# A selective-state mixer and two MLPs: another bank, another order and one work list in the second MLP

## Chip, cores and metric

The kernel runs on one core of one Trainium2 chip, in one launch. The metric is the device time in microseconds, from the first to the last work of an execution. Lower is better.

## What is computed

A chunked state-space mixer (4 batches, 8 heads, 768 steps) gives 3072 tokens of width 256. Two MLPs follow, each from 256 to 2048 and back to 256:

```
h = x @ w_in
g = np.maximum(h, 0.0) + np.log1p(np.exp(-np.abs(h)))      # first MLP: softplus
x = g @ w_out
...
h = x @ w_in
g = h * (1.0 / (1.0 + np.exp(-1.702 * h)))                 # second MLP
return (g @ w_out).astype(np.float32)
```

Inputs and outputs are fp32 in the reference; the weights reach the kernel as 64-bit words.

## The kernel before

**Operands in two parts.** The matrix products run in the type fp32r. A value is kept as a high part (a copy into fp32r) and a low part (the value minus the high part), and a product is three matmuls of 128x128 by 128x512: high by high, and the two mixed ones. Three such matmuls on one output are called a *triple* here. `rnd` makes the high part of an activation on ScalarE (gh), `low` its low part on VectorE (gl).

**First MLP.** The tokens are cut into 6 chunks `c` of 512, the 2048 hidden units into 16 blocks `m`; the loop runs over `t = 16 c + m`, from 0 to 95. A step has `g1` (6 matmuls), a softplus on ScalarE, `rnd`, `low` and, two steps later, `g2` twice (6 matmuls): four triples in all. While chunk c is multiplied, the mixer makes chunk c+1 between these (scans on VectorE, products on TensorE, `at_m` on VectorE after each `at_cb`), up to t = 79; from t = 80 on there is none left.

**Second MLP.** It takes the chunks in pairs `p` (3) and the weights in 8 parts `q`; a *group* `G = 8 p + q` (24 of them) makes the hidden units of one part for two chunks with seven products instead of eight (Strassen's scheme in Winograd's form, with sums of blocks of the weights and of x made beforehand). Each product is a triple. Products 1 and 2 share a PSUM bank: product 1 is copied to `u_p` by ScalarE, then product 2 is added on top of it in the same bank. So product 2 cannot start before the copy has read the bank. VectorE adds: `u_1` = product 6 + `u_p`, `u_2` = product 7 + `u_1`, and in `make` product 5 + `u_2` (called add11 here), product 4 + `u_2` (add10), product 3 on top of 5 + `u_1` (add01). Product 3 goes onto product 5's bank and so waits for add11. `make` then has ScalarE do the activation and `rnd`. `l2()` takes the next entry of a queue: one triple of the second matrix (output sums `o`). Between the products stand `l2` calls: a group has 7 products and 8 `l2`, 15 triples, save the first, which has 13.

**Weight work.** A weight part of the second MLP is a *unit* (16; even ones are w_in parts, "2i", odd ones w_out parts, "2o"). `unit_steps` gives its steps, each for VectorE ("D") or ScalarE ("A"): scale A, three A, join D, sign D, and for 2i block sums and a split in two pieces (4 D and 2 A more), for 2o one split (A, D). `sign` also issues the load of the unit three further on, on SP. The inputs of a pair of chunks have a list of their own (`pair`: differences and splits). `run(jobs, which)` goes through the letters of `which` and, for each, does the next step of the first job whose head is of that engine; before, it looks at the first two unfinished jobs only. Before the change the units 0 and 1 and the first sums of pair 0 start at t = 69 and are brought to their end at t = 80; units 2 to 8 and the rest of pair 0 are run in t = 80 to 95, and what is left is done behind the loop; units 9 to 15 and pair 1 stand in groups 0 to 7, pair 2 in groups 8 on.

Each engine takes its instructions strictly in the order written. `finish` copies an ended output sum, for the second MLP into a buffer `ot`, and SP stores it: a buffer is free again when its store has landed. All `ot` come from one tag with two buffers, which the third difference of a pair uses too.

Of the kernel before, what the change touches and what calls it, by code (L numbers as in the profile page):

```python
# [9 lines left out]
F32 = mybir.dt.float32  # L10
# [11 lines left out]
P = 128  # L22
# [19 lines left out]
def mixer_two_mlps(ctx: ExitStack, tc: tile.TileContext, pack_p, pack_q, pack_s, pack_x, a_rows, consts, w1i, w1o, w2i, w2o, out):  # L42
# [383 lines left out]
    def finish(c, j):  # L426
        if c < NC:
            o = x2[:, c, j, :]
        else:
            o = hid.tile([P, TB], F32, tag="e", name=f"ot{c}_{j}", bufs=2)  # L430
        if j == 0 or c == 2 * NC - 1:
            nc.scalar.activation(o, acc[c][j], AF.Copy)
        else:
            nc.vector.tensor_copy(o, acc[c][j])  # L434
        if c >= NC:
            nc.sync.dma_start(out=out[j, :, (c - NC) * TB : (c - NC + 1) * TB], in_=o)

    W1 = (w1ih, w1il)
    with tc.manual_schedule():
# [228 lines left out]

        def run(jobs, which):
            for eng in which:  # L670
                for job in [j for j in jobs if j][0:2]:
                    if job[0][0] == eng:
                        job.pop(0)[1]()
                        break

        def second():
            second_home()
            low(NT - 1)
            units = [unit_steps(u) for u in range(9, 16)]
            first, then, srcs = pair_sums(1)  # L680
            pair = [first + pair_split(1, then, srcs)]
            queue = [(NT - 2, 0), (NT - 2, 1), (NT - 1, 0), (NT - 1, 1)]
            lo12 = None

            def l2():
                if not queue:
                    return
                t, j = queue.pop(0)
                if t < NT:
                    g2(t, j)  # L690
                    c, last = NC - 1, t % NF == NF - 1
                else:
                    g, f, ct = (t - NT) // 4, (t - NT) // 2 % 2, t % 2
                    d = tt[t]
# [5 lines left out]
                    assert not 4 <= g < 8 or not units[2 * g - 8]  # L700
                    wh, wl = (w2o[n][g % 8][:, f, o] for n in "hl")
                    nc.tensor.matmul(a, wl, d["gh"], start=first, stop=False)  # L702
                    nc.tensor.matmul(a, wh, d["gh"], start=False, stop=False)  # L703
                    nc.tensor.matmul(a, wh, d["gl"], start=False, stop=last)  # L704
                if last:
                    finish(c, j)

            u_p, u_1, u_2 = x2[:, 0, 0], x2[:, 0, 1], x2[:, 1, 0]
            for G in range(24):
# [8 lines left out]
                def bank(n):  # L718
                    return ps_h.tile([P, TB], F32, tag="h", name=f"p{n}_{G}")

                def product(n, dst, start=True):
                    assert not 5 <= G < 8 or not units[2 * q - 9]
# [12 lines left out]
                    rnd(key(f, ct))  # L735
                    queue.extend([(key(f, ct), 0), (key(f, ct), 1)])

                b1 = bank(1)
                product(1, b1)
                nc.scalar.activation(u_p, b1, AF.Copy)  # L740
                if lo12 is not None:
                    low(lo12)
                run(units, "DA")
                l2()
                b6 = bank(6)
                product(6, b6)
                nc.vector.tensor_add(u_1, b6, u_p)
                run(units, "DA")
                run(pair, "DA")
                l2()  # L750
                product(2, b1, start=False)
                make(0, 0, b1)
                if G:
                    l2()
                b7 = bank(7)
                product(7, b7)
                nc.vector.tensor_add(u_2, b7, u_1)  # L757
                low(key(0, 0))
# [16 lines left out]
                run(units, "DA")  # L775
                lo12 = key(0, 1)
                l2()
                l2()
# [4 lines left out]
        for t in range(NT):  # L783
# [79 lines left out]
                first, then, srcs = pair_sums(0)  # L863
                pair = [first + then]
            if t == (NC - 1) * NF:
                for job in (*pair, *units):
                    for _, f in job:
                        f()
                second_open()
                units = [unit_steps(u, nc.vector if u % 2 else nc.scalar) for u in range(2, 9)]  # L870
                pair = [pair_split(0, [], srcs)]
            if c == NC - 2 and m >= 5:
                run(units, "DA" if m % 2 else "DDA")
                run(pair, "D")
# [65 lines left out]
```

## Time and profile before

| | us |
|---|---|
| median of 3 runs | 597.04 (594.16 to 597.46) |
| the profiled execution's own time | 593.67 |
| its span, first to last instruction | 591.9 |
| TensorE busy | 568.9 |
| VectorE busy | 453.5 |
| ScalarE busy | 327.6 |

Rows give times from the start of the span. PE is TensorE, PEld its weight loads, DVE VectorE, ACT ScalarE, SPq the queue of SyncE. A row of the timeline has the start, the duration, the engine, the line, the operation, output and inputs, and in brackets the idle time before it and what ended it. Line L740 is the copy to `u_p`, L726 a product, L702 to L704 an `l2` of the second MLP, L732 the adds of `make`, L734 its activation, L419 `rnd`, L747 and L757 the adds to `u_1` and `u_2`, L811 the softplus, L655 the high part of a weight (`hi`), L122 `scale`, L131 `three`, L136 `join`, L141 `sign`, L432 and L434 `finish`, L83 every subtraction on VectorE.

### The profile page before, as it was taken

Reading aid. Unit: us, or ns where it says so; the run is one execution under the profiler, and the core shown is the slowest. Engines: PE = TensorE matmul, PEld = TensorE weight load, DVE = VectorE, ACT = ScalarE, POOL = GpSimd, SP = SyncE. Lnnn points to the kernel's source line nnn. Section 1 sums busy time; section 2 is a strip of 40 time slices with the busy share of each in tenths; the row PEclk is TensorE's granted clock in tenths of the full one; section 3 lists DMA queues with packets and bytes.
Section 4 is the critical chain, followed back from the end, with each engine's and each line's share of the span. In section 5 each row is a group of like instructions: output and inputs, shape, how many; then the busy total and the mean of one; then the engine's idle time right before and its main releaser. Section 6 shows DMA issues by size and latency. Waiting matters only on the chain.

```text
span 591.9 us, 8940 instructions
## 1 busy us (share of the span) xinstructions
PE 568.9 (96%) x3380; PEld 447.1 (76%) x3380; DVE 453.5 (77%) x686; ACT 327.6 (55%) x560; POOL 104.4 (18%) x95
## 2 busy tenths in 40 slices
PE   7899999999999999999999989999989999999996
PEld 5455667888888888877878767777768888888885
DVE  5999959998787976998688688887566766665654
ACT  2756534544344344544786776675565656564553
POOL 1011336444464443531000000000000000000000
PEclk9799999999999999999999999999999999999999
DMA  8867641433514336221123111000100000100001
GB/s 284 281 191 258 227 161 62 144 114 131 167 47 159 122 124 225 92 93 38 37 83 131 35 37 45 27 0 1 53 18 1 2 0 0 73 1 0 1 1 71
DMA packets 26570, 52.31 MB, mean 88 GB/s; under 512 B 3072, under 2 KB 8608, under 8 KB 26528
## 3 DMA queue, kind: packets, MB, share of 16 engines
q1 hardware_dynamic: 26528, 51.75, 25.6%
q8 instruction: 26, 0.43, 0.3%
q14 instruction: 16, 0.13, 0.1%
HBM read 48.40 MB, written 3.34 MB: 87 GB/s over the span
## 4 chain that ended last, share of the span: by engine, by line
PE 67%; DVE 18%; ACT 7%; DMA 4%; issue 3%; SPq 0%; POOL 0%; DVEq 0%; ACTq 0%; POOLq 0%
PE h L393 15%; PE p L726 15%; PE o L704 5%; PE o L702 5%; PE o L703 5%; PE o L412 4%; PE o L414 4%; PE o L413 4%; PE o L410 3%; DVE gl L83 3%; DVE L L246 2%; ACT gh L419 2%; ACT g L734 2%; DVE g L732 2%; PE y L332 2%
## 5 line engine op out<-in xcount | busy, mean ns | idle before, releaser
L83 DVE TENSOR_TENSOR gl<-g,gh 128x512 fp32r<-128x512 f32 x176 | 139.5, 794 | 32.8 <-ACT gh L419 32.3
L811 ACT ACTIVATE g<-h 128x512 f32<-128x512 f32 x96 | 57.0, 594 | 105.6 <-PE h L393 95.3
L419 ACT ACTIVATE gh<-g 128x512 fp32r<-128x512 f32 x176 | 111.3, 632 | 5.6
L734 ACT ACTIVATE g<-g 128x512 f32<-128x512 f32 x72 | 45.5, 631 | 69.1 <-DVE g L732 67.6
L393 PE MATMUL h<-xh,w1ih 128*128 128x512 f32 x192 | 80.8, 421 | 0.5 <-ACT xh L359 0.5
L393 PE MATMUL h<-xl,w1ih 128*128 128x512 f32 x192 | 76.0, 396 | 0.0
L246 DVE TENSOR_TENSOR_SCAN L<-abz,eye 128x1024 f32<-128x1024 f32 (+1 forms) x25 | 61.8, 2471 | 4.1 <-PE abz L236 4.1
L414 PE MATMUL o<-gl,w1oh 128*128 128x512 f32 x160 | 62.5, 391 | 0.8 <-DVE gl L83 0.8
L412 PE MATMUL o<-gh,w1ol 128*128 128x512 f32 x160 | 63.2, 395 | 0.0
L413 PE MATMUL o<-gh,w1oh 128*128 128x512 f32 x160 | 62.4, 390 | 0.0
L393 PE MATMUL h<-xh,w1il 128*128 128x512 f32 x192 | 60.1, 394 | 0.4 <-DVE w1il L83 0.2
L732 DVE TENSOR_TENSOR g<-p,x 128x512 f32<-128x512 f32 x72 | 48.8, 687 | 11.3 <-PE p L726 10.2
L86 POOL TENSOR_TENSOR rhs_bd<-tc,pk 64x512 fp32r<-64x512 f32 x32 | 53.0, 1657 | 1.2
L702 PE MATMUL o<-gh,w2ol 128*128 128x512 f32 x120 | 46.8, 390 | 0.6 <-DVE ot L434 0.6
L704 PE MATMUL o<-gl,w2oh 128*128 128x512 f32 x120 | 46.7, 389 | 0.0
L703 PE MATMUL o<-gh,w2oh 128*128 128x512 f32 x120 | 46.7, 389 | 0.0
L757 DVE TENSOR_TENSOR x<-p,x 128x512 f32<-128x512 f32 x24 | 16.6, 691 | 35.6 <-PE p L726 35.6
L393 PEld LDWEIGHTS h<-xh,w1ih 128*128 128x128 f32 x192 | 36.3, 189 | 9.8 <-issue 1.9
L393 PEld LDWEIGHTS h<-xl,w1ih 128*128 128x128 f32 x192 | 36.3, 189 | 9.5 <-issue 2.9
L393 PEld LDWEIGHTS h<-xh,w1il 128*128 128x128 f32 x192 | 36.2, 189 | 9.1 <-DVE w1il L83 1.2
L311 DVE TENSOR_TENSOR L<-cb,L 128x512 f32<-128x512 f32 x40 | 26.8, 680 | 12.6 <-PE cb L301 12.6
L414 PEld LDWEIGHTS o<-gl,w1oh 128*128 128x128 f32 x160 | 30.0, 188 | 8.0 <-DVE gl L83 1.7
(164 smaller groups left out, 1043.0 us busy)
## 6 DMA issues: line engine op xcount, KB each, us to landing
abz<-scr_z SPq DMA_DIRECT2D x22, 512.0 KB, 4.0
pk<-pack_s SPq DMA_DIRECT2D x16, 512.0 KB, 4.6
px<-pack_x SPq DMA_DIRECT2D x20, 320.0 KB, 2.9
wraw_1i<-w1i SPq DMA_DIRECT2D x8, 512.0 KB, 4.4
wraw_1o<-w1o SPq DMA_DIRECT2D x8, 512.0 KB, 4.2
wraw_2i<-w2i SPq DMA_DIRECT2D x8, 512.0 KB, 3.5
wraw_2o<-w2o SPq DMA_DIRECT2D x8, 512.0 KB, 3.2
out<-ot SPq DMA_DIRECT2D x12, 256.0 KB, 2.0
```

Of the source, the lines that this page charges most:

```text
L83: nc.vector.tensor_sub(o, x, y)
L246: nc.vector.tensor_tensor_scan(out=d["L"][:, h].rearrange("p h t -> p (h t)"), data0=d["abz"][:, h].rearrange("p h t -> p (h t)"), data1=e ...
L393: nc.tensor.matmul(h, w[:, k, f], x[:, k, :], start=(n == 0), stop=(n == 5))
L412: nc.tensor.matmul(a, w1ol[:, m, o], d["gh"], start=first, stop=False)
L413: nc.tensor.matmul(a, w1oh[:, m, o], d["gh"], start=False, stop=False)
L414: nc.tensor.matmul(a, w1oh[:, m, o], d["gl"], start=False, stop=last)
L419: nc.scalar.activation(d["gh"], d["g"], AF.Copy)
L702: nc.tensor.matmul(a, wl, d["gh"], start=first, stop=False)
L703: nc.tensor.matmul(a, wh, d["gh"], start=False, stop=False)
L704: nc.tensor.matmul(a, wh, d["gl"], start=False, stop=last)
L726: nc.tensor.matmul(dst, w, x, start=start and i == 0, stop=i == 2, skip_group_check=not start)
L732: nc.vector.tensor_add(d["g"], src, add)
```

## The change

Four things, all in the order or the place of work; the matmuls are the same ones.

1. Product 1 of a group gets a bank of its own (pool `ps_c`, one bank, which the mixer used before), and product 7 comes ahead of product 2: the order of products goes from 1, 6, 2, 7, 5, 4, 3 to 1, 6, 7, 2, 5, 4, 3. `low` of the first activation comes behind add11.
2. Weight and pair work of the second MLP is taken from one list at set places of a group (`behind`), in the groups 0 and 1 from all units, from group 2 on from the first unit, the pair, the second unit. `run` looks at the whole list it is given.
3. In the first MLP the work starts at t = 77 instead of 69, with 3 VectorE and 2 ScalarE steps in each t up to 95; nothing is brought to its end at t = 80. All `scale` steps are on ScalarE. What is left of the units goes on in the second MLP. The table of the activation is loaded ahead of group 0.
4. `finish`: every j = 1 copy is VectorE's and goes to another tag (two buffers); the very last copy is cut in two halves of 256 columns, one on VectorE and one on ScalarE, each with its own store.

```diff
             o = x2[:, c, j, :]
         else:
-            o = hid.tile([P, TB], F32, tag="e", name=f"ot{c}_{j}", bufs=2)
-        if j == 0 or c == 2 * NC - 1:
-            nc.scalar.activation(o, acc[c][j], AF.Copy)
-        else:
-            nc.vector.tensor_copy(o, acc[c][j])
...
+            pool, tag = (hid, "e") if j == 0 else (stg, "wt")
+            o = pool.tile([P, TB], F32, tag=tag, name=f"ot{c}_{j}", bufs=2)
+        parts = [slice(0, TB)] if (c, j) != (2 * NC - 1, 1) else [slice(0, TB // 2), slice(TB // 2, TB)]
+        for i, f in enumerate(parts):
+            if j == i:
+                nc.scalar.activation(o[:, f], acc[c][j][:, f], AF.Copy)
+            else:
+                nc.vector.tensor_copy(o[:, f], acc[c][j][:, f])
...
         def run(jobs, which):
             for eng in which:
-                for job in [j for j in jobs if j][0:2]:
-                    if job[0][0] == eng:
+                for job in jobs:
+                    if job and job[0][0] == eng:
...
-        def second():
+        def second(units):
             second_home()
+            nc.scalar.preload_act_table(AF.Gelu_apprx_sigmoid)
             low(NT - 1)
-            units = [unit_steps(u) for u in range(9, 16)]
+            units = units + [unit_steps(u) for u in range(len(units) + 2, 16)]
...
+            def behind(which):
+                jobs = [j for j in units if j]
+                run([*jobs[0:1], *pair, *jobs[1:2]] if G >= 2 else jobs, which)
...
-                b1 = bank(1)
+                b1 = ps_c.tile([P, TB], F32, tag="cb", name=f"p1_{G}")
                 product(1, b1)
                 nc.scalar.activation(u_p, b1, AF.Copy)
+                behind("D")
                 if lo12 is not None:
                     low(lo12)
-                run(units, "DA")
+                behind("AA")
                 l2()
                 b6 = bank(6)
                 product(6, b6)
+                behind("D")
                 nc.vector.tensor_add(u_1, b6, u_p)
-                run(units, "DA")
-                run(pair, "DA")
+                behind("DA")
+                l2()
+                b7 = bank(7)
+                product(7, b7)
+                nc.vector.tensor_add(u_2, b7, u_1)
+                behind("DADAD")
                 l2()
                 product(2, b1, start=False)
                 make(0, 0, b1)
                 if G:
                     l2()
-                b7 = bank(7)
-                product(7, b7)
-                nc.vector.tensor_add(u_2, b7, u_1)
-                low(key(0, 0))
-                run(units, "DAD")
-                l2()
                 b5 = bank(5)
                 product(5, b5)
+                behind("A")
                 make(1, 1, b5, u_2)
+                low(key(0, 0))
...
             if t == (NC - 1) * NF:
-                for job in (*pair, *units):
-                    for _, f in job:
-                        f()
                 second_open()
-                units = [unit_steps(u, nc.vector if u % 2 else nc.scalar) for u in range(2, 9)]
-                pair = [pair_split(0, [], srcs)]
-            if c == NC - 2 and m >= 5:
-                run(units, "DA" if m % 2 else "DDA")
-                run(pair, "D")
-            if c == NC - 1:
-                run(units, "DADA" if m % 2 else "DADAD")
-                run(pair, "DA")
-        for job in (*units, *pair):
-            for _, f in job:
-                f()
-        second()
+                pair[0] += pair_split(0, [], srcs)
+                units += [unit_steps(u) for u in range(2, 9)]
+            if t >= (NC - 1) * NF - 3:
+                run([*[u for u in units if u][0:1], *pair, *[u for u in units if u][1:2]], "DADAD")
...
+        second(units[2:])
```

How the order moves, first on ScalarE between the roundings of group 2 and the first activation of group 3 (`x2_100<-p1_3` is the copy to `u_p`). Before:

```order
L734 ACTIVATE g2_01_3772<-g2_01_3772 128x512
L419 ACTIVATE gh105_3775<-g2_01_3772 128x512
L655 ACTIVATE w1oh_98<-wt_2o5_3617 128x512
L740 ACTIVATE x2_100<-p1_3_3786 128x512
L131 ACTIVATE wraw_2i6_3547<-wraw_2i6_3547 128x512
L122 ACTIVATE wt_2o6_3804<-wraw_2o6_3641 128x512
L583 ACTIVATE w1oh_98<-t3_1_3509 128x512
L734 ACTIVATE g3_00_3813<-p1_3_3786 128x512
```

With the change:

```order
L745 ACTIVATE g2_01_3773<-g2_01_3773 128x512
L419 ACTIVATE gh105_3776<-g2_01_3773 128x512
L751 ACTIVATE x2_100<-p1_3_3786 128x512
L131 ACTIVATE wraw_2o6_3628<-wraw_2o6_3628 128x512
L658 ACTIVATE w1ih_96<-x2_100 128x512
L658 ACTIVATE w1ih_96<-sums_367 128x384
L745 ACTIVATE g3_00_3828<-p1_3_3786 128x512
```

The weight split that stood between the rounding and the copy to `u_p` now stands behind the copy.

Second, VectorE from a step behind the last add of group 0 to add11 of group 1 (`g1_11<-p5_1`). With the change:

```order
L141 SCALAR_TENSOR_TENSOR x2_100<-wraw_2o4_3397,x2_100 128x512
L83 TENSOR_TENSOR gl97_3601<-g0_01_3578,gh97_3581 128x512
L83 TENSOR_TENSOR w2ol_3106<-x2_100,w2oh_3104 128x512
L760 TENSOR_TENSOR x2_100<-p6_1_3611,x2_100 128x512
L136 SCALAR_TENSOR_TENSOR wt_2i5_3534<-wt_2i5_3534,wraw_2i5_3448 128x512
L765 TENSOR_TENSOR x2_100<-p7_1_3622,x2_100 128x512
L141 SCALAR_TENSOR_TENSOR wt_2i5_3534<-wraw_2i5_3448,wt_2i5_3534 128x512
L641 TENSOR_TENSOR sums_367<-wt_2i5_3534 128x128
L83 TENSOR_TENSOR wt_2i5_3534<-wt_2i5_3534 128x128
L83 TENSOR_TENSOR sums_367<-sums_367,wt_2i5_3534 128x128
L83 TENSOR_TENSOR sums_367<-wt_2i5_3534,sums_367 128x128
L743 TENSOR_TENSOR g1_11_3654<-p5_1_3649,x2_100 128x512
```

All weight steps of a group now stand ahead of add11, where before some stood among the adds that follow it, as in the next group of the kernel before:

```order
L732 TENSOR_TENSOR g2_11_3746<-p5_2_3742,x2_100 128x512
L732 TENSOR_TENSOR g2_10_3758<-p4_2_3754,x2_100 128x512
L83 TENSOR_TENSOR gl107_3763<-g2_11_3746,gh107_3749 128x512
L83 TENSOR_TENSOR w1ol_99<-x2_100,w1oh_98 128x512
L732 TENSOR_TENSOR g2_01_3772<-p5_2_3742,x2_100 128x512
```

Third, the last copies on ScalarE, with the semaphores each waits for. Before:

```order
L734 ACTIVATE g23_01_5552<-g23_01_5552 128x512 [waits DVE_49]
L419 ACTIVATE gh189_5555<-g23_01_5552 128x512 [waits PE_49,Activation_49]
L432 ACTIVATE ot10_0_5576<-o10_0_4995 128x512 [waits DMAHW2_49,PE_49]
L432 ACTIVATE ot11_0_5588<-o11_0_5010 128x512 [waits DMAHW4_49,PE_49,Activation_49]
L432 ACTIVATE ot11_1_5594<-o11_1_5011 128x512 [waits DMAHW3_49,DMAHW1_49,DMAHW5_49,DVE_49,PE_49]
```

With the change:

```order
L745 ACTIVATE g23_01_5553<-g23_01_5553 128x512 [waits DVE_49]
L419 ACTIVATE gh189_5556<-g23_01_5553 128x512 [waits PE_49,Activation_49]
L435 ACTIVATE ot10_0_5577<-o10_0_4996 128x512 [waits DMAHW0_49,PE_49]
L435 ACTIVATE ot11_0_5589<-o11_0_5011 128x512 [waits DMAHW2_49,PE_49]
L435 ACTIVATE ot11_1_5595<-o11_1_5012 128x256 [waits DMAHW7_49,DMAHW3_49,DVE_49]
```

The buffers of the last copies are now those of stores two output chunks earlier, and ScalarE's half of the last copy waits for VectorE, whose half stands first.

## Rows read from the trace of the kernel before

**Rows 1.** The page's part 1: busy time, share of the span, instructions.

```profile
PE 568.9 (96%) x3380; PEld 447.1 (76%) x3380; DVE 453.5 (77%) x686; ACT 327.6 (55%) x560; POOL 104.4 (18%) x95
```

**Rows 2.** Windows of 20 us in the second MLP: busy us (instructions), granted clock, DMA.

```profile
340.00:360.00 20.00, 17.78 (x76) 14.05 (x77) 16.11 (x28) 13.77 (x25) 0.00 (x0) 1.00 0.13 46
440.00:460.00 20.00, 20.00 (x90) 16.55 (x89) 13.14 (x21) 12.07 (x20) 0.00 (x0) 1.00 0.00 1
```

**Rows 3.** Waits of TensorE: us in total, times, longest.

```profile
PE p L726 <- ACT x L740: 6.0, 8, 1.4
PE cb L301 <- DVE L L311: 1.6, 2, 0.9
PE p L726 <- DVE g L732: 1.4, 2, 0.9
...
PE o L414 <- DVE gl L83: 0.8, 1, 0.8
```

**Rows 4.** Timeline, group 1: a weight split, the copy to `u_p`, product 2.

```profile
339.94 0.61 ACT L655 ACTIVATE w2oh<-x 128x512 fp32r<-128x512 f32 x1
...
340.46 0.58 ACT L740 ACTIVATE x<-p 128x512 f32<-128x512 f32 x1
...
341.09 0.50 PE L726 MATMUL p<-x2h,w2ih 128*128 128x512 f32 x1 [1.13 <-ACT x L740]
```

**Rows 5.** Timeline: product 1 of group 0, product 2 of group 3, product 1 of group 10, `u_p` twice.

```profile
327.05 0.39 PE L726 MATMUL p<-x2h,w2ih 128*128 128x512 f32 x1
...
364.00 0.50 PE L726 MATMUL p<-x2h,w2ih 128*128 128x512 f32 x1 [0.46 <-ACT x L740]
...
439.84 0.39 PE L726 MATMUL p<-x2h,w2ih 128*128 128x512 f32 x1
...
471.74 0.58 ACT L740 ACTIVATE x<-p 128x512 f32<-128x512 f32 x1
481.94 0.58 ACT L740 ACTIVATE x<-p 128x512 f32<-128x512 f32 x1
```

**Rows 6.** Timeline, VectorE in group 9: the copy of an output sum.

```profile
429.07 0.69 DVE L434 COPY ot<-o 128x512 f32<-128x512 f32 x1 [1.66 <-DMA out<-ot]
```

**Rows 7.** Timeline, ScalarE: the softplus of t = 55, 63, 79 and 95.

```profile
204.59 0.60 ACT L811 ACTIVATE g<-h 128x512 f32<-128x512 f32 x1 [2.46 <-PE h L393]
...
229.55 0.60 ACT L811 ACTIVATE g<-h 128x512 f32<-128x512 f32 x1 [2.46 <-PE h L393]
...
281.23 0.60 ACT L811 ACTIVATE g<-h 128x512 f32<-128x512 f32 x1 [2.53 <-PE h L393]
...
325.88 0.60 ACT L811 ACTIVATE g<-h 128x512 f32<-128x512 f32 x1 [0.96 <-PE h L393]
```

**Rows 8.** Timeline, ScalarE in group 0: `three`, the table load, the first activation.

```profile
328.97 0.65 ACT L131 ACTIVATE wraw_2o<-wraw_2o 128x512 uint32<-128x512 uint8 x1
329.64 1.28 ACT L734 ACT_TABLE_LOAD   x1
330.93 0.60 ACT L734 ACTIVATE g<-p 128x512 f32<-128x512 f32 x1
```

**Rows 9.** Timeline, VectorE: a block sum at t = 82, and two operations in group 1.

```profile
289.35 0.29 DVE L638 TENSOR_TENSOR sums<-wt_2i 128x128 f32<-128x128 f32 x1
...
340.67 0.68 DVE L83 TENSOR_TENSOR w2ol<-x,w2oh 128x512 fp32r<-128x512 f32 x1
341.27 0.68 DVE L747 TENSOR_TENSOR x<-p,x 128x512 f32<-128x512 f32 x1
```

**Rows 10.** Timeline at the end: TensorE's last matmul and the last copy.

```profile
586.49 0.39 PE L704 MATMUL o<-gl,w1oh 128*128 128x512 f32 x1
...
588.40 0.60 ACT L432 ACTIVATE ot<-o 128x512 f32<-128x512 f32 x1 [0.17 <-DMA out<-ot]
```

**Rows 11.** Loads of weights: the page's part 6, and all loads of line L110.

```profile
wraw_2i<-w2i SPq DMA_DIRECT2D x8, 512.0 KB, 3.5
...
DMA to landing us min/median/max: 3.1/3.8/9.2
```

More of the change, by code (lines that the diff above doesn't have):

```diff
@@ L429, in finish @@
         else:
-            o = hid.tile([P, TB], F32, tag="e", name=f"ot{c}_{j}", bufs=2)
-        if j == 0 or c == 2 * NC - 1:
-            nc.scalar.activation(o, acc[c][j], AF.Copy)
-        else:
-            nc.vector.tensor_copy(o, acc[c][j])
-        if c >= NC:
-            nc.sync.dma_start(out=out[j, :, (c - NC) * TB : (c - NC + 1) * TB], in_=o)
+            pool, tag = (hid, "e") if j == 0 else (stg, "wt")
[6 more added lines that the diff above has]
+                nc.vector.tensor_copy(o[:, f], acc[c][j][:, f])
+            if c >= NC:
+                nc.sync.dma_start(out=out[j, :, (c - NC) * TB + f.start : (c - NC) * TB + f.stop], in_=o[:, f])
     W1 = (w1ih, w1il)
@@ L670, in run, with ready @@
             for eng in which:
-                for job in [j for j in jobs if j][0:2]:
-                    if job[0][0] == eng:
+                for job in jobs:
+                    if job and job[0][0] == eng:
                         job.pop(0)[1]()
                         break
-        def second():
+        def second(units):
             second_home()
+            nc.scalar.preload_act_table(AF.Gelu_apprx_sigmoid)
             low(NT - 1)
-            units = [unit_steps(u) for u in range(9, 16)]
+            units = units + [unit_steps(u) for u in range(len(units) + 2, 16)]
             first, then, srcs = pair_sums(1)
             pair = [first + pair_split(1, then, srcs)]
+            def ready(u):
+                return not units[u - 2]
+            def behind(which):
+                jobs = [j for j in units if j]
+                run([*jobs[0:1], *pair, *jobs[1:2]] if G >= 2 else jobs, which)
             queue = [(NT - 2, 0), (NT - 2, 1), (NT - 1, 0), (NT - 1, 1)]
@@ L699, in l2 @@
                     last = g % 8 == 7 and f != ct
-                    assert not 4 <= g < 8 or not units[2 * g - 8]
+                    assert not 1 <= g < 8 or ready(2 * g + 1)
                     wh, wl = (w2o[n][g % 8][:, f, o] for n in "hl")
@@ L721, in product @@
                 def product(n, dst, start=True):
-                    assert not 5 <= G < 8 or not units[2 * q - 9]
+                    assert not 1 <= G < 8 or ready(2 * q)
                     wh, wl = (w2i[x][q][:, BLOCK[n] * P : BLOCK[n] * P + P] for x in "hl")
@@ L774, in second @@
                 low(key(1, 0))
-                run(units, "DA")
                 lo12 = key(0, 1)
@@ L865, in mixer_two_mlps @@
             if t == (NC - 1) * NF:
-                for job in (*pair, *units):
-                    for _, f in job:
-                        f()
                 second_open()
-                units = [unit_steps(u, nc.vector if u % 2 else nc.scalar) for u in range(2, 9)]
-                pair = [pair_split(0, [], srcs)]
-            if c == NC - 2 and m >= 5:
-                run(units, "DA" if m % 2 else "DDA")
-                run(pair, "D")
-            if c == NC - 1:
-                run(units, "DADA" if m % 2 else "DADAD")
-                run(pair, "DA")
-        for job in (*units, *pair):
-            for _, f in job:
-                f()
-        second()
+                pair[0] += pair_split(0, [], srcs)
+                units += [unit_steps(u) for u in range(2, 9)]
+            if t >= (NC - 1) * NF - 3:
+                run([*[u for u in units if u][0:1], *pair, *[u for u in units if u][1:2]], "DADAD")
+        import sys; print("AT END", len(pair[0]), [len(u) for u in units], file=sys.stderr)
+        for _, f in pair[0]:
+            f()
+        assert not units[0] and not units[1]
+        second(units[2:])
     ps_ctx.close()
```

## The prediction

> **What bounds the kernel now.** The page's first part shows TensorE busy 568.9 of 591.9 us [rows 1], so the kernel is bound by TensorE, and a gain can only come from stretches in which it waits, and from the two ends. The windows say where: in the second MLP it is busy 17.78 of 20 us between 340 and 360 and all of 20 between 440 and 460, at the full granted clock (1.00, the 2.4 GHz level) in both [rows 2]. TensorE's own waits name the releaser: eight waits, 6.0 us, for the copy to `u_p`, two for add11 or add01, and three in the first MLP for VectorE [rows 3]. The timeline of one shows why: a weight split stands on ScalarE ahead of the copy, and product 2 starts as the copy ends [rows 4].
>
> **What the stretch loses.** Between two copies of the steady part lie 10.20 us [rows 5], for 15 triples: 0.68 each. From product 1 of group 0 to that of group 10 the matmuls alone need 13 x 0.68 + 9 x 10.20 = 100.64 us; the trace has 439.84 - 327.05 = 112.79 [rows 5]. The loss is 12.15 us, more than the idle time in the waits, since a wait also empties the matmul pipeline (the first matmul behind it takes 0.50 us instead of 0.39 [rows 4, 5]).
>
> In the first MLP eight steps take 24.96 us (t = 55 to 63), so t = 63 to 79 should take 49.92 and took 51.68; t = 79 to 95 should take 16 x 4 x 0.68 = 43.52 and took 44.65 [rows 7]. That is 1.76 + 1.13 = 2.89 us lost there.
>
> **The change: groups 3 to 23.** Product 2 now starts 6 triples (4.08 us) into a group instead of 4 (2.72), and the copy no longer has a split ahead of it. Where VectorE is not late, product 3 of the group before starts at 8.16 and its sum is ready 0.89 later (0.45 to the start of its third matmul, 0.39 for that, 0.04 to the next engine), at 9.05; add01, activation, rounding and the copy follow in 0.6 to 0.7 us each, and the copy ends about 1.5 us into the next group: 2.5 us to spare. The next deadline is product 3, which starts 12 triples (8.16 us) into a group and needs add11. In front of add11 VectorE has up to 10 operations of a start-to-start 0.60 us (340.67 to 341.27) and four small ones of 0.3 [rows 9]. I laid the order of the built program on these durations. In group 3 add11 starts at 6.5 and is ready at 7.2, in group 4 (pair 1's split of 1024 columns) at 7.5, in group 8 (pair 2 and a copy of an output sum) at 7.9: all before 8.16. So no loss from group 3 on. The waits for stores in groups 8 and 9 (VectorE stood 1.66 us [rows 6]) go with the second tag. The new bank for product 1 is read last by the first activation, about 5.6 us into a group, and wanted again at 10.2.
>
> **Groups 0 to 2** carry most weight work, and are late in the new order too.
> Group 0 (0 is its product 1): ScalarE ends `three` of unit 8 at 0.8, the table at 2.05, the copy at 2.7; two splits, a `scale` and a `three` follow at 0.45 to 0.55 start to start, until 4.7. VectorE does join, sign and gl of t = 95 from 0.8, four sums to 3.7, `u_1`, `u_2`, two low parts, a join, and starts add11 at 6.6, ready 7.3. Product 3 could start after 10 triples, 6.8: 0.5 late, with 0.1 for the pipeline 0.6.
> Group 1: add01 of group 0 starts at 0.6 (VectorE waits for roundings before it), gl 1.2, sign 1.8, gl 2.7, low 3.75 (it waits for ScalarE's split), `u_1`, join, `u_2`, sign each 0.6 on, four sums to 7.85, then add11, ready 8.6 against 8.16: 0.5 lost.
> Group 2: likewise ready 8.5: 0.4 lost.
> Left: 1.5 us, so the gain here is 12.15 - 1.5 = 10.6. Bounds: 12.15, and 7 if groups 0 to 2 stay as they are (a rival, below).
>
> **First MLP.** With nothing brought to its end at t = 80 and VectorE free for the mixer until t = 77, the two waits on `at_m` go. At t = 78 `at_m` is still behind three moved steps, one of which waits for ScalarE's `three`; I get it ready 5.4 us after t = 77 began and wanted at 6.1. From t = 80 on a step has 2.72 us. VectorE has one gl and three steps, about 2.4 (4 x 0.60), ScalarE softplus, rounding and two steps, about 2.5, now with the three scales that VectorE did. Each load of a unit is issued some six steps ahead of its use, against 3.5 us to land [rows 11]. Both fit, but barely, and each can hold the other up, so I leave 0.5 of the 2.89: gain 2.4. Bounds: 2.9 and 0.
>
> **The end.** TensorE ends at 586.88; the last copy starts only at 588.40, behind stores, and ends at 589.0 [rows 10]. With the new tags it waits for no store. The halves do not run side by side: ScalarE's waits for VectorE's in the built order. Between 0.29 us for 128 columns and 0.69 for 512 [rows 6, 9] I take 0.4 for each, so the last ends at 587.75: gain 1.25. Bounds: 1.5 and 0.5. The stores behind it I leave as they are.
>
> **The table load** costs 1.28 us wherever it stands; before, it stood between product 2 and the first activation, now ahead of the copy, and is in the times of group 0 above. In the row it starts 0.02 us after the `three` before it ended, and the activation follows 0.01 us after it [rows 8].
> The Trainium skill, "ScalarE: Activation LUTs", section "What ACT_TABLE_LOAD costs", adds a drain of about 1.38 us to each load, 2.66 in all. By that the whole of ScalarE's list in group 0 would come 1.38 later.
>
> **Sum.** 10.6 + 2.4 + 1.25 = 14.2 us. Against the profiled execution's 593.67 that gives 579.5; the median shown is 3.4 above that execution, so 597.04 - 14.2 = 582.8.
>
> **Rivals.**
> 1. *VectorE and ScalarE stay too full at the seam.* For it: in the first MLP's last chunk both have 2.4 to 2.5 of 2.72 us, and every wait between them stops all that is queued behind. Then t = 77 to 95 and groups 0 to 2 lose what they lose now. Product 2 of group 3 stands at 364.00 [rows 5] and without waits at 327.05 + 8.84 + 20.40 + 2.72 = 359.01, so 5.0 of the 12.15 stay; the gain is 7.15 + 1.25 = 8.4: 588.6.
> 2. *A load lands late.* In group 1 ScalarE is to scale unit 12, whose load is issued by the sign of unit 9 in the same group (ready 2.5), with the activations of the group queued behind. At 3.5 us to landing [rows 11] the first rounding is ready at 8.5, wanted at 8.84, so past about 3.9 each us costs one. At the 9.2 of the slowest load [rows 11], which came in the busy first part of the kernel, that is 5.3: 588.1.
> 3. *The load of the table empties ScalarE first*, ahead of the copy and of all that is queued behind it. If that took as long as the load itself, 1.28 us [rows 8], and all of it came through to groups 0 and 1: 584.1. Against it: there is no such time in [rows 8]. The Trainium skill's rule on the drain, named above, is this rival.
> 4. *Slower: one bank for all first products.* Product 1 of each of 23 groups waits for the activation of the group before, where three rotating banks served. It decides from 10.2 us on; I find that activation at 5.6, in the early groups up to 7.2. To end 3 us above the median it would have to cost (14.2 + 3) / 23 = 0.75 us a group, so to end 5 us later than I find.
> 5. *No better than now*: that the change would not do what it says is ruled out by the order, in which the split stands behind the copy.
>
> **How the numbers follow.** Forecast 0.68, rival 1 0.17, rival 2 0.06, rival 3 0.05, rival 4 0.04. About 0.5% (3 us) is what a measurement of this kernel can tell from no change. Of rivals 1 and 2, 0.07 end within it, where new waits add to them. Faster: 0.68 + 0.05 + 0.16 = 0.89; same 0.07; slower 0.04. The range: with nothing lost anywhere the gain is 12.15 + 2.89 + 1.5 = 16.5, so 580.5, and the runs shown lie more below their median than above it, so 579.0; on the other side it takes in rivals 1 to 3 with some more, 589.5.
>
> **What would show it.** Right: no wait of TensorE for the copy to `u_p` from group 3 on, 10.2 us from group to group from there, waits of some tenths for add11 in groups 0 to 2, none on `at_m` in t = 72 to 77, the last copy ending within 0.9 us of the last matmul. Wrong: waits for add11 or a rounding in groups 3 to 9, gaps for gl in t = 80 to 95, ScalarE idle before a `scale` in group 1.

## The result and the profile after

The changed kernel took 580.4 us (median of 4 runs, 578.62 to 581.24) beside 595.78 for the kernel before (median of 4, 594.16 to 597.46): a ratio of 0.9738, 95% interval 0.9695 to 0.9781. Measured again later, it took 582.79 beside 597.51, with a ratio of 0.9754 (0.9728 to 0.9781). The forecast was 582.8, faster. It was reckoned down from 597.04, the median of the three runs that were shown; a fourth run lowered it.

Executions of one kernel begin at different paces (last section), so stretches are compared inside a trace. From the softplus of t = 63 to the end of the span the kernel before took 591.9 - 229.55 = 362.35 us [rows 7] and the changed one 579.4 - 231.40 = 348.0: 14.35 us less. Spans are shown to a tenth of a us, so the last digit of what is reckoned from one is uncertain. The 15.4 us between the two medians hold the start of the executions too.

Here are the page's part 1, then windows of 20 us (span; busy us and instructions of PE, PEld, DVE, ACT, POOL; granted clock, DMA share, GB/s), answering to [rows 1] and [rows 2]:

```profile
PE 568.5 (98%) x3380; PEld 452.7 (78%) x3380; DVE 453.1 (78%) x684; ACT 331.6 (57%) x563; POOL 102.4 (18%) x95
```

```profile
320.00:340.00 20.00, 19.49 (x86) 15.82 (x85) 16.05 (x29) 17.02 (x30) 0.00 (x0) 1.00 0.20 68
340.00:360.00 20.00, 19.03 (x82) 14.74 (x81) 17.68 (x32) 14.57 (x26) 0.00 (x0) 1.00 0.20 65
360.00:380.00 20.00, 20.00 (x90) 16.57 (x89) 19.00 (x33) 16.32 (x29) 0.00 (x0) 1.00 0.09 27
```

TensorE does the same 568 us of work in a shorter span. In the last of these windows it is never idle, though VectorE is busier there (19.00 of 20) than where TensorE waits. Of TensorE's waits (us in total, times, longest) the groups of [rows 3] on the copy, on `at_m` and on gl are gone; one is left of the second MLP:

```profile
PE p L737 <- DVE g L743: 1.5, 3, 0.6
```

These are product 3 waiting for add11 in groups 0, 1 and 2. In the timeline stand product 1 of group 0, the three waits, then product 1, the copy and product 2 of group 3, and product 1 of group 10:

```profile
325.38 0.39 PE L737 MATMUL p<-x2h,w2ih 128*128 128x512 f32 x1
...
332.86 0.73 PE L737 MATMUL p<-xo,w2ih 128*128 128x512 f32 x2 [0.51 <-DVE g L743]
...
343.96 0.73 PE L737 MATMUL p<-xo,w2ih 128*128 128x512 f32 x2 [0.61 <-DVE g L743]
...
355.09 0.73 PE L737 MATMUL p<-xo,w2ih 128*128 128x512 f32 x2 [0.36 <-DVE g L743]
...
357.26 0.39 PE L737 MATMUL p<-x2h,w2ih 128*128 128x512 f32 x1
...
358.93 0.58 ACT L751 ACTIVATE x<-p 128x512 f32<-128x512 f32 x1
...
361.34 0.39 PE L737 MATMUL p<-x2h,w2ih 128*128 128x512 f32 x1
...
428.66 0.39 PE L737 MATMUL p<-x2h,w2ih 128*128 128x512 f32 x1
```

In group 3 the copy ends at 359.51 and product 2 starts at 361.34, 4.08 us after product 1: 1.8 us to spare where [rows 4] show none. Product 1 of group 0 to that of group 10 (called *the ten groups* below) takes 428.66 - 325.38 = 103.28 us, against 112.79 in [rows 5]: 9.51 less. The softplus of t = 63, 79 and 95, answering to [rows 7]:

```profile
231.40 0.60 ACT L822 ACTIVATE g<-h 128x512 f32<-128x512 f32 x1 [2.46 <-PE h L393]
...
280.70 0.60 ACT L822 ACTIVATE g<-h 128x512 f32<-128x512 f32 x1 [0.80 <-PE h L393]
...
324.22 0.60 ACT L822 ACTIVATE g<-h 128x512 f32<-128x512 f32 x1 [0.38 <-PE h L393]
```

49.30 and 43.52 us, before 51.68 and 44.65: 3.51 less. At the end the two halves of the last copy, answering to [rows 10]:

```profile
575.32 0.39 PE L715 MATMUL o<-gl,w1oh 128*128 128x512 f32 x1
575.74 0.43 DVE L437 COPY ot<-o 128x256 f32<-128x256 f32 x1 [0.67 <-PE o L715]
576.20 0.38 ACT L435 ACTIVATE ot<-o 128x256 f32<-128x256 f32 x1 [0.54 <-DVE ot L437]
```

From TensorE's end to the end of the span pass 579.4 - 575.71 = 3.69 us instead of 591.9 - 586.88 = 5.02: 1.33 less. 9.51 + 3.51 + 1.33 = 14.35, the whole difference.

### The profile page after: what moved, and what is told of

Read it like the earlier page. It is cut to its first block, busy times and chain, and to the rows that moved or that the text cites. A ratio compares the mean times of both kernels' runs of the same rounds, so it can differ in the third digit from the quotient of the medians.

```text
span 579.4 us, 8939 instructions
## 1 busy us (share of the span) xinstructions
PE 568.5 (98%) x3380; PEld 452.7 (78%) x3380; DVE 453.1 (78%) x684; ACT 331.6 (57%) x563; POOL 102.4 (18%) x95
## 4 chain that ended last, share of the span: by engine, by line
PE 87%; DVE 7%; ACT 3%; issue 2%; DMA 1%; POOL 0%; DVEq 0%; POOLq 0%; ACTq 0%; SPq 0%
PE h L393 20%; PE p L737 17%; PE o L713 7%; PE o L714 7%; PE o L715 7%; PE o L412 6%; PE o L413 6%; PE o L414 6%; PE o L410 3%; PE y L332 2%; PE cb L277 2%; DVE L L246 2%; PE cb L301 1%; PE y L323 1%; PE abz L236 1%
## 5 line engine op out<-in xcount | busy, mean ns | idle before, releaser
L246 DVE TENSOR_TENSOR_SCAN L<-abz,eye 128x1024 f32<-128x1024 f32 (+1 forms) x25 | 63.3, 2534 | 3.9 <-PE abz L236 3.9
L745 ACT ACTIVATE g<-p 128x512 f32<-128x512 f32 x24 | 14.3, 594 | 49.9 <-PE p L737 49.8
L412 PEld LDWEIGHTS o<-gh,w1ol 128*128 128x128 f32 x160 | 30.0, 188 | 6.8 <-ACT gh L419 0.4
```

The costliest lines, as they stand in the source:

```text
L246: nc.vector.tensor_tensor_scan(out=d["L"][:, h].rearrange("p h t -> p (h t)"), data0=d["abz"][:, h].rearrange("p h t -> p (h t)"), data1=e ...
L412: nc.tensor.matmul(a, w1ol[:, m, o], d["gh"], start=first, stop=False)
L745: nc.scalar.activation(d["g"], src, AF.Gelu_apprx_sigmoid)
```

## The experiments

Times of single runs differ by some us from start to start, so verdicts rest on the stretches.

**1. The old order of products back.**

```diff
+                product(2, b1, start=False)
+                make(0, 0, b1)
+                if G:
+                    l2()
                 b7 = bank(7)
...
-                product(2, b1, start=False)
-                make(0, 0, b1)
-                if G:
-                    l2()
```

> The change with the old order of products (1, 6, 2, 7, 5, 4, 3); bank and work list stay new. Measured on the stretch from product 1 of group 0 to product 1 of group 10 (103.3 us in the changed kernel, 112.8 before). Theory, that the early copy to u_p or the late product 2 is enough, each alone: from group 3 on the copy ends 1.5 us into a group against 2.72 for product 2, so no wait for the copy there; but product 7 and u_2 come 1.36 us later, and add11 with them by up to 0.7: 104 to 106 us, with waits for add11. Rival, that the order of products is what brought the gain: waits for the copy in most of groups 1 to 7, 109 us or more.

The ten groups took 105.58 us, 2.30 more, within what the theory gave. As it had it, TensorE's waits are for add11, and none for the copy is long enough to be listed:

```profile
PE p L737 <- DVE g L743: 2.8, 4, 1.0
```

Groups 0 to 3 together take 42.1 us, as in the changed kernel; of the 2.30 us, 0.63 lie in group 4 and 1.53 in groups 8 and 9, where the next pair's work stands.

**2. Two ScalarE steps ahead of the copy again, in the new order.**

```diff
                 product(1, b1)
+                behind("AA")
                 nc.scalar.activation(u_p, b1, AF.Copy)
...
-                behind("AA")
```

> The change with the two ScalarE steps of the work list ahead of the copy to u_p instead of behind it; order of products and bank stay new. Theory: the copy ends 0.5 to 1.2 us later, still before product 2 at 4.08 us into the group: within 0.8 us of the changed kernel's 103.3 us for groups 0 to 9, no waits for the copy from group 3 on. Rival, that the place of the steps is what brought the gain: waits for the copy of 0.4 to 1.1 us in groups 1 to 7, 107 us or more.

The ten groups took 104.12 us, 0.84 more, a little over what was allowed. There is one wait for the copy (0.54 us, group 1), the wait for add11 in group 0 has grown to 1.09, and there is nothing from group 3 on:

```profile
PE p L737 <- DVE g L743: 1.1, 1, 1.1
PE p L737 <- ACT x L752: 0.5, 1, 0.5
```

**3. Both undone.**

The two diffs together.

> The change with both undone: old order of products and two ScalarE steps ahead of the copy; the bank and the rest of the list stay new. Theory: the waits for the copy come back in groups 1 to 7, and the stretch of groups 0 to 9 takes 107 to 111 us. Rival, that the waits went for another reason (fewer VectorE steps among the adds, the bank): 104 to 106 us, as with the old order alone.

The ten groups took 107.68 us, 4.40 more, where the two alone sum to 3.14. The waits for the copy are back, but only three (groups 0, 1, 3), not one in each of groups 1 to 7:

```profile
PE p L737 <- ACT x L752: 2.7, 3, 1.4
PE p L737 <- DVE g L743: 1.3, 2, 0.9
```

So either remedy alone removes most of the waits: more time for the copy, or nothing in front of it. But with both undone the ten groups still take 5.11 us less than in the kernel before, so the rest of the change (the tag, the list and what it holds) has that much of the gain without the order; its parts are not told apart here.

**4. Product 1 back in the three rotating banks.**

```diff
-                b1 = ps_c.tile([P, TB], F32, tag="cb", name=f"p1_{G}")
+                b1 = bank(1)
```

> The change with product 1 back in the three rotating banks, nothing else undone. Theory, that the bank alone brings nothing: with three banks product 5 takes the bank of product 6, product 4 that of product 7, both read long before, and the next product 1 its own bank again: groups 0 to 9 within 0.5 us of the changed kernel's 103.3. Rival, that the bank is what brought the gain: a wait for an add or an activation in each group, 106 us or more, also in the groups from 10 on, which take 10.20 us each now.

The ten groups took 103.32 us, with the same three waits (1.4 us together). In the changed kernel the bank of its own brings nothing, and rival 4, by which it would cost, falls too.

**5. One tag for the output copies.**

```diff
-            pool, tag = (hid, "e") if j == 0 else (stg, "wt")
-            o = pool.tile([P, TB], F32, tag=tag, name=f"ot{c}_{j}", bufs=2)
+            o = hid.tile([P, TB], F32, tag="e", name=f"ot{c}_{j}", bufs=2)
```

> All copies of ended output sums of the second MLP go back to one tag with two buffers; the halves of the last copy stay. Theory (the second tag removed waits for stores in groups 8 and 9 and at the end): VectorE waits for a store again in group 8 or 9, product 1 of group 8 to that of group 10 takes 21.4 to 23.9 us instead of 20.40, and from the last matmul to the end of the span 4.4 to 5.2 us instead of 3.7; the whole 1.7 to 5 us more than the changed kernel. Rival (with the new order nothing waits for those copies, the tag matters at the end at most): 20.4 to 20.8 us for the two groups, the end within 0.3 us of the changed kernel's.

Product 1 of group 8 to that of group 10 took 430.90 - 408.47 = 22.43 us (20.40), and the end 583.0 - 577.94 = 5.06 (3.69): 2.0 and 1.4 us more, as the theory said. VectorE stands still for a store in group 9 and once more at the end:

```profile
421.12 0.69 DVE L436 COPY ot<-o 128x512 f32<-128x512 f32 x1 [2.26 <-DMA out<-ot]
...
421.87 0.50 PE L712 MATMUL o<-gh,w2ol 128*128 128x512 f32 x1 [0.62 <-DVE ot L436]
...
579.49 0.42 DVE L436 COPY ot<-o 128x256 f32<-128x256 f32 x1 [2.18 <-DMA out<-ot]
```

**6. The first MLP's weight work at its old places.**

```diff
             if t == (NC - 1) * NF:
+                for job in (*pair, *units):
+                    for _, f in job:
+                        f()
                 second_open()
-                pair[0] += pair_split(0, [], srcs)
-                units += [unit_steps(u) for u in range(2, 9)]
-            if t >= (NC - 1) * NF - 3:
-                run([*[u for u in units if u][0:1], *pair, *[u for u in units if u][1:2]], "DADAD")
...
-        for _, f in pair[0]:
-            f()
...
-        second(units[2:])
+                units = [unit_steps(u, nc.vector if u % 2 else nc.scalar) for u in range(2, 9)]
+                pair = [pair_split(0, [], srcs)]
+            if c == NC - 2 and m >= 5:
+                run([j for j in units if j][0:2], "DA" if m % 2 else "DDA")
+                run(pair, "D")
+            if c == NC - 1:
+                run([j for j in units if j][0:2], "DADA" if m % 2 else "DADAD")
+                run(pair, "DA")
+        for job in (*units, *pair):
+            for _, f in job:
+                f()
+        second([[] for _ in range(7)])
```

> The weight work of the first MLP stands as in the kernel before (from t = 69, brought to its end at t = 80 and behind the loop, odd scales on VectorE); the second MLP is the changed one. Theory (the first MLP's loss came from this placement alone): t = 63 to 79 takes 51.2 to 51.8 us instead of 49.30, t = 79 to 95 takes 44.2 to 44.8 instead of 43.52; product 1 of group 0 to that of group 10 takes 102.0 to 103.6 instead of 103.28, as less work is left for groups 0 to 2; the whole 1.5 to 4 us more. Rival (the loss lay with the seam, where both engines are full either way): t = 63 to 95 within 0.8 us of the changed kernel's 92.82, and groups 0 to 2 lose more.

The softplus of t = 63, 79 and 95:

```profile
231.74 0.60 ACT L822 ACTIVATE g<-h 128x512 f32<-128x512 f32 x1 [2.46 <-PE h L393]
...
283.44 0.60 ACT L822 ACTIVATE g<-h 128x512 f32<-128x512 f32 x1 [2.55 <-PE h L393]
...
328.09 0.60 ACT L822 ACTIVATE g<-h 128x512 f32<-128x512 f32 x1 [0.96 <-PE h L393]
```

t = 63 to 79 took 51.70 us and 79 to 95 took 44.65, the old values: the whole gain of the first MLP comes from this placement, and the rival of a full seam falls. The second half missed: the ten groups took 104.17 us, not less than 103.28. Less work is left, but none of it is begun: in group 0 VectorE stands 2.31 us for the first `three`, which comes behind the table load on ScalarE, and TensorE then waits 1.23 us for add11:

```profile
332.39 0.69 DVE L136 SCALAR_TENSOR_TENSOR x<-x,wraw_2o 128x512 uint32<-128x512 uint32 x1 [2.31 <-ACT wraw_2o L131]
```

**7. In group 1 only the first two units in the list.**

```diff
-                run([*jobs[0:1], *pair, *jobs[1:2]] if G >= 2 else jobs, which)
+                run([*jobs[0:1], *pair, *jobs[1:2]] if G >= 2 else jobs[0:2] if G else jobs, which)
```

> In group 1 the list holds the first two unfinished units only, so that no scale of unit 12 stands on ScalarE there. Theory (add11 of groups 0 to 2 is late because VectorE has too many steps ahead of it): ScalarE waits for no load in group 1, but TensorE still waits for add11 there; product 1 of group 1 to that of group 2 takes 10.9 to 11.4 us (11.36 in the changed kernel), product 1 of group 0 to that of group 10 102.7 to 103.4. Rival (ScalarE's wait for the load, 1.32 us, holds up the roundings and so everything): 10.2 to 10.6 us for group 1 and at most 102.5 in all.

In the changed kernel ScalarE does wait in group 1 for the load of unit 12, as rival 2 had it:

```profile
341.45 0.68 ACT L122 ACTIVATE x<-wraw_2i 128x512 f32<-128x512 f32 x1 [1.32 <-DMA wraw_2i<-w2i]
```

Without that wait (this run) the ten groups take 103.31 us, group 1 alone 11.36, and TensorE's waits are 0.51, 0.60 and 0.36 as before. The late load is real and costs nothing here.

**8. One VectorE step moved behind add10 in groups 0 to 2** (with the list of experiment 7).

```diff
-                behind("DADAD")
+                behind("DADA" if G < 3 else "DADAD")
...
                 make(1, 0, b4, u_2)
+                if G < 3:
+                    behind("D")
```

> As the kernel with two units in group 1, and in groups 0 to 2 one VectorE step is moved from ahead of product 2 to behind add10, so behind add11. Theory (VectorE's list ahead of add11): add11 comes 0.6 us earlier in each of groups 0 to 2; product 1 of group 0 to that of group 10 takes 101.0 to 102.2 us instead of 103.28, and the time falls by 1.1 to 2.3 us against the changed kernel. Rival (the step that is moved makes add01 and the next copy late by as much): 102.9 to 104.0, and waits of TensorE for the copy in groups 1 to 3.

The theory failed: the ten groups took 103.23 us, in the rival's range; the time was 582.53, a ratio of 0.976 to the kernel before (0.9722 to 0.9799), so not to be told from the changed kernel. TensorE waits for add11 once, for 0.38 us, but group 1 now takes 349.44 - 337.77 = 11.67. What it waits on is next in line, ScalarE's queue in group 1:

```profile
345.84 0.63 ACT L658 ACTIVATE w1ih<-wt_2i 128x512 fp32r<-128x512 f32 x1 [2.69 <-DVE wt_2i L83]
346.38 0.58 ACT L745 ACTIVATE g<-p 128x512 f32<-128x512 f32 x1
...
347.67 0.50 PE L713 MATMUL o<-gh,w2ol 128*128 128x512 f32 x1 [0.23 <-ACT gh L419]
```

The split of a weight waits 2.69 us for VectorE's block sums, and the first activation is queued behind it: it starts 8.61 us into the group (346.38 - 337.77), and an l2 waits for its rounding. The long wait itself is not new: with the step at its old place (experiment 7) it is 2.68 us, and the activation starts 8.31 us into the group, as in the changed kernel (343.35 - 335.04).

```profile
345.69 0.63 ACT L658 ACTIVATE w1ih<-wt_2i 128x512 fp32r<-128x512 f32 x1 [2.68 <-DVE wt_2i L83]
346.23 0.58 ACT L745 ACTIVATE g<-p 128x512 f32<-128x512 f32 x1
```

What the move adds is 0.30 us in the activation's place. The rival's waits for the copy did not come.

**9. The same step left out of groups 0 to 2 and done in groups 3 to 7** (with the list of experiment 7).

```diff
-                behind("DADAD")
+                behind("DADA" if G < 3 else "DADAD")
```

> As the kernel with two units in group 1, and in each of groups 0 to 2 one VectorE step less is done at all ahead of product 2; the three steps are done in groups 3 to 7. Theory (VectorE has more to do in groups 0 to 2 than 10.20 us hold, so a step must leave the group, not only change its place in it): TensorE's waits for add11 there (0.52, 0.60, 0.36) go or stay under 0.15 each, product 1 of group 0 to that of group 10 takes 100.7 to 101.6 us instead of 103.28, and the stretch from the softplus of t = 63 to the end of the span 345.6 to 346.5 instead of 348.0. Rival (the list has no room in groups 3 to 7, where VectorE is busy 9.5 to 9.9 of 10.2 us): new waits for add11 there, 102.4 to 104.

No wait for add11 is left in TensorE's list. Product 1 of groups 0 and 10:

```profile
325.90 0.39 PE L737 MATMUL p<-x2h,w2ih 128*128 128x512 f32 x1
...
427.34 0.39 PE L737 MATMUL p<-x2h,w2ih 128*128 128x512 f32 x1
```

The ten groups take 101.44 us, 0.80 from the ideal, and from t = 63 to the end 578.1 - 231.91 = 346.2, as the theory said. The time was 579.95 us, a ratio of 0.9714 (0.9685 to 0.9744). Groups 3 to 7 had room: each takes 10.20 us.

**10. TensorE's pause at 6 us filled** (on top of experiment 9).

```diff
             at_spread_a(0, ac[2], half)
+            for _ in range(3 if half == 0 else 0):
+                nc.tensor.matmul(idle[:, 0:T], wz, wz, start=True, stop=True)
```

> As the kernel with fewer steps, and three more matmuls of zeros in TensorE's pause of 1.39 us at about 6 us, ahead of the second half of the first spread of the mixer. Theory (in some executions TensorE comes out of this pause at half its pace: twelve matmuls of 96x256 take 5.49 us instead of 2.86, and all that follows comes 2.7 us later): with the pause filled, the twelve take 2.86 us; the softplus of t = 63 stands at 231.0 to 232.0 us in the profiled execution, and the times of all executions spread by less than 2 us, against 5.7 in the kernel with the moved step. Rival (the pace has nothing to do with the pause): the times spread as before, or the start comes later by up to 0.5 us.

The time was 577.82 us, a ratio of 0.9679 (0.9653 to 0.9706), the shortest median here, though its interval overlaps that of experiment 9. From t = 63 to the end the two are alike (575.4 - 229.21 = 346.2), so what differs is the start. Its four runs lie within 1.9 us (577.18 to 579.08), those of experiment 9 within 5.5 (577.01 to 582.52). The softplus of t = 63 stands at 229.21, earlier than expected:

```profile
229.21 0.60 ACT L824 ACTIVATE g<-h 128x512 f32<-128x512 f32 x1 [2.46 <-PE h L393]
```

**11. The order and the bank alone, on the kernel before.**

```diff
-                b1 = bank(1)
+                b1 = ps_c.tile([P, TB], F32, tag="cb", name=f"p1_{G}")
...
+                b7 = bank(7)
+                product(7, b7)
+                nc.vector.tensor_add(u_2, b7, u_1)
+                run(units, "DAD")
+                l2()
                 product(2, b1, start=False)
                 make(0, 0, b1)
                 if G:
                     l2()
-                b7 = bank(7)
-                product(7, b7)
-                nc.vector.tensor_add(u_2, b7, u_1)
-                low(key(0, 0))
-                run(units, "DAD")
-                l2()
...
                 make(1, 1, b5, u_2)
+                low(key(0, 0))
```

> The kernel before, with two things of the change alone: the bank of its own for product 1, and product 7 ahead of product 2 (the low part of the first activation then stands behind add11). The weight work stays at its places, a split still stands ahead of the copy in some groups. Theory (the order gives the copy 4.08 us instead of 2.72, and that is what most groups lacked): TensorE's waits for the copy fall from 6.0 us to at most 1.5, and product 1 of group 0 to that of group 10 takes 108.0 to 110.2 us instead of 112.79; the waits for stores in groups 8 and 9 stay. Rival (VectorE, whose steps still stand among the adds, is late next): the waits for add11 or add01 grow by as much as the copy's fall, 111 to 113.

Far more than expected: the ten groups took 432.31 - 329.18 = 103.13 us, so order and bank alone (and the bank brings nothing in experiment 4) give 9.66 us of the ten groups, as much as the whole change gives. In group 1 the split still stands ahead of the copy, and product 2 is held up by 0.2 us:

```profile
341.60 0.62 ACT L655 ACTIVATE w2oh<-x 128x512 fp32r<-128x512 f32 x1
...
342.12 0.58 ACT L740 ACTIVATE x<-p 128x512 f32<-128x512 f32 x1
...
342.75 0.50 PE L726 MATMUL p<-x2h,w2ih 128*128 128x512 f32 x1
```

No wait for the copy or for add11 is long enough to be listed among TensorE's waits. Groups 0 to 2 take 9.27, 10.57 and 10.20 us, 0.80 over the ideal, where the changed kernel loses 2.64; groups 8 and 9 lose 1.69 to stores.

Set beside this run, the changed kernel's 14.35 us are 9.66 for the order, 1.69 and 1.33 for the stores and the end, and 3.51 in the first MLP, less 1.84 that groups 0 to 2 lose more (2.64 against 0.80) with the weight work that the first MLP no longer does. By experiment 3 the parts overlap, so another sequence of steps would share them out otherwise.

Experiment 6 leaves the second MLP the same work as this run (units 9 to 15, pair 1), and there groups 0 to 3 lose 3.53 us. So for that work the old places were better than the new list with the table load ahead of group 0; these two are not told apart.

**12. The changed kernel again, beside 9 to 11.**

> The changed kernel itself, timed beside the kernels with fewer steps on the same chip. The theories agree that its stretches repeat: 103.28 us from product 1 of group 0 to that of group 10, 348.0 from the softplus of t = 63 to the end of the span. The median should lie 1.5 to 2.5 us above that of the kernel with fewer steps if that one's stretch is down to 101.6 or less, and within 1 us of it if not.

The ten groups took 103.32 us, t = 63 to the end 581.5 - 233.43 = 348.1. Its median of 582.79 is 2.84 above that of experiment 9, more than the 1.5 to 2.5 expected. The stretches show 1.9 of it; the rest is not from them, and is put down to the start (last section).

## Why the prediction was right, point by point

**What bounds the kernel** held: the work on TensorE is unchanged, and each us gained is a us that it no longer waits.

**Groups 3 to 23** were forecast without loss and have none: 10.20 us from group to group, no wait for the copy, and add11 in time in groups 3, 4 and 8. Experiment 11 shows the cause stronger than it was put: the 4.08 us to product 2 are enough even with a split ahead of the copy, but for 0.2 us in group 1, so that placing the split behind it mattered little once the order had changed (0.84 us in experiment 2). Experiments 1 and 3 show why undoing the order alone cost only 2.30: with nothing ahead of the copy the 2.72 us nearly do.

**Groups 0 to 2: the term that was mis-sized.** "Left: 1.5 us" measured 2.64 (0.82, 1.16, 0.66). The place and the cause were right: add11, behind VectorE's list. Two parts were small. Product 3 started 0.68, 0.76 and 0.53 us late (332.86 against 325.38 + 6.80, 343.96 against 335.04 + 8.16, 355.09 against 346.40 + 8.16) where 0.5, 0.45 and 0.35 were laid out. In group 1 the list was late from its start: add01 of group 0 was put at 0.6 us into it and starts at 0.94 (335.98 - 335.04). And the pipeline was put at 0.1 a wait: in group 0 the matmul behind the wait's first two comes 0.11 us late, and in group 1 a late rounding, with the low part behind it, stretches the next triples by another 0.3. The idle time in the waits list shows only 1.5 of the 2.64, since it is counted from the modelled end of a matmul, 0.16 us after the next could have started. So the second MLP's gain was 9.51, not 10.6, and experiment 9 beside 8 shows what would have taken most of it back: a step less in the group, not a place behind add10 in it. Six VectorE steps ahead of add11 do not fit there; with five (experiment 9) or, in group 1 of experiment 11, four, 0.80 us is left in all.

**First MLP: mis-sized the other way.** Forecast 2.4, bound 2.89; measured 3.51. The loss of 2.89 was counted against 24.96 us for eight steps, taken ahead of t = 63, where TensorE has more to do for the mixer: 201 matmuls in those eight steps, 337 in the sixteen that follow (in the changed kernel's windows, without an idle moment in either). So t = 63 to 79 takes 49.30 without loss, not 49.92, and the bound should have been 3.51. The 0.5 left for two full engines did not come.

**The two sizes cancel**: 1.1 us too much there, 1.1 too little here; the sum was 14.2 and measures 14.35, which is luck as far as these two go. **The end**: forecast 1.25, measured 1.33, with ScalarE's half waiting 0.54 us for VectorE's, as the order had it. The stores in groups 8 and 9 went with the second tag, and would cost 2.0 us there without it (experiment 5).

**The rivals.** 1, the full seam, falls (experiment 6). 2, the late load, was there, 1.32 us, and cost nothing (experiment 7). 4 falls (experiment 4). 3, the emptying of ScalarE at the table load, has no row:

```profile
325.39 0.64 ACT L131 ACTIVATE wraw_2i<-wraw_2i 128x512 uint32<-128x512 uint8 x1
326.05 1.28 ACT L681 ACT_TABLE_LOAD   x1
...
327.34 0.60 ACT L751 ACTIVATE x<-p 128x512 f32<-128x512 f32 x1
```

The load starts 0.02 us after the step before it and the copy 0.01 us after the load, so the switch takes its 1.28 us and no more. The drain of about 1.38 us of the Trainium skill, "ScalarE: Activation LUTs", section "What ACT_TABLE_LOAD costs", is not in this trace.

## What to carry to other kernels

Where a matmul must wait for another engine to read its bank, first move independent products into the gap: here that reorder, made alone on the kernel before, brought as much of the ten groups as the whole change, and it made the place of the work ahead of the copy matter less (0.84 us, against 2.10 in the old order). Count an engine's steps ahead of each deadline: here a step too many had to leave the group, and the one other place in it that was tried only made the next queue late. Take the length without loss from the stretch in question, not from one that does other work.

## What was not expected of the hardware

Executions of one kernel differ by up to 5.7 us (578.49 to 584.17 in experiment 8), and where profiles of like kernels differ, they do so at the start. After a pause of 1.39 us TensorE does the work of six fp32 matmuls, which the profile counts as twelve of 96x256, in 2.86 us or in 5.49. First the changed kernel's profile, then that of experiment 12, the same kernel:

```profile
6.92 2.86 PE L236 MATMUL abz<-ac,cc 96*128 96x256 f32 x12 [1.39 <-DVE L L246]
```

```profile
7.08 5.49 PE L236 MATMUL abz<-ac,cc 96*128 96x256 f32 x12 [1.39 <-DVE L L246]
```

The second row is 1.9 times as long, and its softplus of t = 63 stands 2.0 us later; four of the fourteen profiles have it (experiments 1, 7, 8 and 12). The changed kernel's profile is slowed too, only later, after a pause of 1.74 us at 12 us. From 15 to 20 us both are at the slow pace: the same sixteen matmuls take 1.08 us in the changed kernel and in experiment 12, and 0.64 in experiment 10.

```profile
19.17 1.08 PE L332 MATMUL y<-L,x 128*32 128x128 f32 x16
```

```profile
16.68 1.08 PE L332 MATMUL y<-L,x 128*32 128x128 f32 x16
```

```profile
16.58 0.64 PE L332 MATMUL y<-L,x 128*32 128x128 f32 x16
```

The granted clock of that stretch doesn't tell it: it reads 0.50, the lower of the two levels (1.2 GHz), in the changed kernel (first window), but 1.00 in experiment 12 (second), where the rows are as slow.

```profile
15.00:20.00 5.00, 5.00 (x56) 3.52 (x49) 4.97 (x7) 2.56 (x5) 0.41 (x1) 0.50 0.93 340
```

```profile
15.00:20.00 5.00, 5.00 (x54) 3.42 (x55) 4.78 (x6) 1.20 (x3) 0.38 (x1) 1.00 0.60 229
```

With the pause half filled (0.72 us left) experiment 10's profile has 2.86:

```profile
4.87 0.83 PE L471 MATMUL idle<-wz 128*128 128x128 f32 x6
6.42 2.86 PE L236 MATMUL abz<-ac,cc 96*128 96x256 f32 x12 [0.72 <-DVE L L246]
```

The mean granted clock of a whole execution sorts the fourteen profiles: with 0.990 to 0.994 the softplus of t = 63 stands at 229.2 to 230.6 us (3 profiles), with 0.981 to 0.988 at 231.4 to 231.9 (7), with 0.996 to 1.000 at 233.0 to 234.4 (4). All four runs of experiment 10 have 0.990 to 0.994, of experiment 9's six only one (0.993), of the changed kernel's nine two. That speaks for filling the pause. But experiment 10's one profile was at the faster pace ahead of the pause already (its first four records of L236 take 1.25 us, 1.75 in the changed kernel's profile), as are the two others of its kind (1.43 and 1.35), so it isn't settled.
